# Attention and gated MLP for one decoded token: q made in groups along the steps, W_o in four sets, W_down by plain columns

## The chip, the cores and the metric

The kernel runs on one core of one Trainium2 chip. The metric is device time in microseconds (us) of the whole launch, as the median of several runs. An engine name in what follows is the profile's: PE is TensorE's matmul, PEld its weight load, DVE is VectorE, ACT is ScalarE, POOL is GpSimd, SP is SyncE, which here only issues DMAs.

## The reference, cut to what matters

One token for each of B = 2 sequences goes through a pre-normalised attention with a cache, then through a gated MLP. Everything is bf16 at the interface.

```python
B, D = 2, 512;  Hq = Hkv = 32;  Sk = 8192;  Dh = 128;  F = 1376
q = layernorm(x) @ wq                                # (2, 512) @ (512, 4096)
p = softmax(q . k_cache * Dh**-0.5)                  # per sequence and head, 8192 keys
h = x + concat_heads(p . v_cache) @ wo               # (2, 4096) @ (4096, 512)
n = layernorm(h)
out = h + (relu(n @ W_gate) * (n @ W_up)) @ W_down   # 512 -> 1376 -> 512
```

The two caches hold 2 x 32 x 8192 x 128 elements each, 134 MB apiece. The weights are 4 MB each for wq and wo, and 1.4 MB for each of the three MLP matrices.

## The kernel before, in words

**Steps.** One step handles two heads of one sequence; there are N = 32 steps (`steps`, 16 pairs of heads for each sequence). A step's keys are one 4 MB load, 128 partitions of 128 keys (64 partitions for each head), into one of two slots of `kbuf`; its values are another into one of two slots of `vbuf` (`load_kv`, L118). The order of instructions is written out by hand: each engine runs its own in the order of the code, and all big loads are issued by SP in that order.

**Scores** (`scores`, L255). Of the 128 keys of a partition, 112 are done by DVE: a multiply with the replicated query `qrep` (L290), four halving adds (L297) and a sum (L301). The other 16 go over PE: transposes (L275), copies by ACT (L276), matmuls with `qT` (L266). Then come the row maxima (`pm`, L309), a matmul that spreads them (`mx_ps`, L311), `nm` (L316) and the exponentials on ACT (L319), which write `pgz`. The next step's multiply stands behind `nm` in DVE's order.

**Values** (`values`, L324). The values of step i-1 stand behind the scores of step i on PE: 32 matmuls of 512 columns (L344), or, in the last three steps, 128 matmuls of 128 rows (L333). Every fourth step a group of heads is collected and normalised into `ocol`.

**Loop** (L362 to L369). Step i: `scores(i)`, the load of K(i+2) into the slot that step i has just read, `values(i-1)`, the load of V(i+1) into the slot that those values have read. So a K load is issued when DVE and PE are done with a step's keys, a V load when PE is done with the values.

**Before the loop.** x is normalised, wq is loaded into `wbig`, and q is made in eight groups of four heads (L206 to L214): four matmuls of 512 columns (`q_ps`, L209), a copy by ACT (`qrow`, L213), four matmuls that replicate it over the partitions (`r_ps`, L200), a copy by ACT (`qrep`, L204). After all eight groups, 32 small matmuls make `qT` (L217), and only then come the transposes of step 0 in PE's order.

**After the loop.** SP issues W_o (L377, three pieces of one layout: partition p holds 32 consecutive rows of W_o), W_gate and W_up (L384, into `kbuf` slot 0), W_down (L388, L393, into tiles of its own). Then come the last scores, with the values of step 30 between, the values of step 31, the spreading of `ocol` into W_o's row layout (L407 on DVE, L411 on PE, `orow` L415), 128 matmuls with W_o (L420; the weights are columns at a stride of four elements), the second layernorm (L428 to L436, L456), the two products (L450), `gate` and `hm` (L463, L469), 44 matmuls with W_down (L476, stride four), the residual (L481), four matmuls that turn columns into rows (L485), two copies (L488, L489) and the output DMA (L490).

Of the kernel before, what the change touches and what calls it, by code (L numbers as in the profile page):

```python
# [7 lines left out]
ACT = mybir.ActivationFunctionType  # L8
ALU = mybir.AluOpType
# [14 lines left out]
def kernel(  # L24
# [25 lines left out]
    NG = Hq // 2  # L50
# [6 lines left out]
    bf16 = mybir.dt.bfloat16  # L57
    f32 = mybir.dt.float32

    FULL = F // (2 * P) * 2  # L60
# [1 line left out]
    FC = FULL + 1  # L62


    SETS = [(0, Hq, P, (16, 12, 4))]

    WD = (3, 1, 1)

# [3 lines left out]
    big = ctx.enter_context(tc.tile_pool(name="big", bufs=1))  # L72
    consts = ctx.enter_context(tc.tile_pool(name="consts", bufs=1))
# [5 lines left out]
    pad = big.tile([P, 192], bf16)  # L79
    kbuf = big.tile([P, 2, ROW], bf16)  # L80
    vbuf = big.tile([P, 2, ROW], bf16)
    wbig = big.tile([P, KC * Hq * Dh], bf16)
    wd_sb = big.tile([P, FULL, D], bf16)
    wd_r = big.tile([P, D], bf16)

    wq_sb = wbig.rearrange("p (c n) -> p c n", c=KC)
    wgu = kbuf[:, 0, 0:2 * KC * F].rearrange("p (k c f) -> p k c f", k=2, c=KC)

    qrep = consts.tile([P, B, NG, Dh], bf16)
    qrow = consts.tile([P, Hq * Dh], bf16)  # L90
# [1 line left out]
    zc = consts.tile([P, B, NG, 2], f32)  # L92
    ob = consts.tile([P, T4 * Dh], f32)
    ident = consts.tile([P, P], bf16)
    identf = consts.tile([P, P], f32)
    nscale = consts.tile([P, P], f32)
    ones = consts.tile([P, P], f32)
    mean_w = consts.tile([P, P], f32)
# [2 lines left out]
    eps_col = consts.tile([P, 1], f32)  # L101
    warm = consts.tile([P, 1], f32)
    ocol = consts.tile([P, Hq, B], bf16)
    rows = [m * Dh // pn for _, m, pn, _ in SETS]
    quot = [consts.tile([P, Dh // n], bf16, name=f"quot{k}") for k, n in enumerate(rows)]
    rest = [consts.tile([P, n], bf16, name=f"rest{k}") for k, n in enumerate(rows)]
    orow = [consts.tile([P, n, B], bf16, name=f"orow{k}") for k, n in enumerate(rows)]
# [10 lines left out]
    def load_kv(cache, buf, i, pieces=1):  # L118
        b, g = steps[i]
        w = ROW // pieces  # L120
        for k in range(pieces):
            nc.sync.dma_start(
                out=buf[:, i % 2, k * w:(k + 1) * w],
                in_=_dram(cache, (b * Hkv + 2 * g) * Sk * Dh + k * w, [[ROW, P], [1, w]]),
            )
# [12 lines left out]

    with tc.manual_schedule():

        nc.sync.dma_start(out=wbig, in_=_dram(A_wq, 0, [[KC * Hq * Dh, P], [1, KC * Hq * Dh]]))
        nc.scalar.dma_start(out=xrow[0:B, :], in_=_dram(A_x, 0, [[D, B], [1, D]]))
        load_kv(A_k_cache, kbuf, 0, pieces=2)
        load_kv(A_k_cache, kbuf, 1)
# [10 lines left out]
        nc.gpsimd.memset(pgz, 0.0)  # L155
        nc.gpsimd.memset(zc, 0.0)
        nc.gpsimd.memset(ob, 0.0)
        nc.gpsimd.memset(identf, 0.0)
        select(identf, 1.0, 0, [[-1, P]], 1)

        nc.gpsimd.memset(sel, 0.0)
        for j in range(2):
# [30 lines left out]
        nc.scalar.activation(out=warm, in_=eps_col, func=ACT.Exp)  # L193


        def spread(n):
            r_ps = ps2.tile([P, B, 2, Dh], f32, tag="tp", name="r_ps")
            for b in range(B):
                for j in range(2):
                    nc.tensor.matmul(  # L200
                        out=r_ps[j * HALF:(j + 1) * HALF, b], lhsT=pick[0:B, b, :],
                        rhs=_free(qrow[0:B, :], (4 * n + j) * Dh, [[2 * Dh, 2], [1, Dh]]), start=True, stop=True,
                    )
            nc.scalar.activation(out=qrep[:, :, 2 * n:2 * n + 2, :], in_=r_ps, func=ACT.Copy)  # L204

        for n in range(NG // 2):  # L206
            q_ps = ps2.tile([P, 512], f32, tag="tp")
            for c in range(KC):
                nc.tensor.matmul(  # L209
                    out=q_ps[0:B, :], lhsT=xn[:, c, :], rhs=wq_sb[:, c, n * 512:(n + 1) * 512],  # L210
                    start=(c == 0), stop=(c == KC - 1),
                )
            nc.scalar.activation(out=qrow[0:B, n * 512:(n + 1) * 512], in_=q_ps[0:B, :], func=ACT.Copy)  # L213
            spread(n)  # L214
        qT_ps = ps.tile([P, Hq, B], f32, tag="acc")
        for h in range(Hq):
            nc.tensor.matmul(  # L217
                out=qT_ps[:, h, :], lhsT=qrow[0:B, h * Dh:(h + 1) * Dh], rhs=ident[0:B, 0:B],
                start=True, stop=True,
            )  # L220
        nc.scalar.activation(out=qT, in_=qT_ps, func=ACT.Copy)


        groups = {}
# [137 lines left out]
        for i in range(N - 1):  # L362
            scores(i)
            if i + 2 < N:
                load_kv(A_k_cache, kbuf, i + 2)
            if i >= 1:
                values(i - 1)
            if i + 1 < N:
                load_kv(A_v_cache, vbuf, i + 1, pieces=2 if i + 1 == N - 1 else 1)  # L369

        off = 0
        wo_at = []
        for (h0, m, pn, pieces), n in zip(SETS, rows):
            wo_at.append(off)
            r0 = 0
            for w in pieces:
                nc.sync.dma_start(  # L377
                    out=wbig[0:pn, off + r0 * D:off + (r0 + w) * D],
                    in_=_dram(A_wo, h0 * Dh * D + r0 * D, [[n * D, pn], [1, w * D]]),
                )  # L380
                r0 += w
# [17 lines left out]


        att_ps = ps.tile([P, KC, B], f32, tag="acc")
        for k, (h0, m, pn, _) in enumerate(SETS):
            n = rows[k]
            or_ps = ps.tile([P, B, n], f32, tag="mx")
            for b in range(B):
                sp = small.tile([P, m, Dh // n], bf16, tag="spread")
                nc.vector.tensor_tensor(  # L407
                    out=sp, in0=_free(ocol, h0 * B + b, [[B, m], [0, Dh // n]]),
                    in1=_free(quot[k], 0, [[0, m], [1, Dh // n]]), op=ALU.mult,
                )  # L410
                nc.tensor.matmul(  # L411
                    out=or_ps[0:pn, b, :], lhsT=sp.rearrange("p h q -> p (h q)"), rhs=rest[k],
                    start=True, stop=True,
                )
            nc.vector.tensor_copy(orow[k][0:pn], or_ps[0:pn].rearrange("p b c -> p c b"))  # L415
        for k, (h0, m, pn, _) in enumerate(SETS):
            n = rows[k]
            for r in range(n):
                for c in range(KC):
                    nc.tensor.matmul(  # L420
                        out=att_ps[:, c, :],
                        lhsT=_free(wbig[0:pn, :], wo_at[k] + r * D + c, [[KC, P]]), rhs=orow[k][0:pn, r, :],
                        start=(k == 0 and r == 0 and c == 0),
                        stop=(k == len(SETS) - 1 and r == n - 1), skip_group_check=True,
                    )
# [35 lines left out]
        for r, f in parts:  # L461
            nf = f.stop - f.start
            nc.vector.scalar_tensor_tensor(  # L463
                out=gate[r, f, :], in0=g_ps[r, f, :], scalar=0.0, in1=_free(rvar[r], 0, [[0, nf], [1, B]]),
                op0=ALU.max, op1=ALU.mult,
            )
        product(u_ps, 1)
# [4 lines left out]
        d_ps = ps2.tile([P, KC, B], f32, tag="o")  # L472
        for fc in range(FC):
            w, src = (P, wd_sb[:, fc, :]) if fc < FULL else (LASTW, wd_r[0:LASTW])
            for c in range(KC):
                nc.tensor.matmul(  # L476
                    out=d_ps[:, c, :], lhsT=_free(src, c, [[KC, P]]), rhs=hm[0:w, fc, :],
                    start=(fc == 0 and c == 0), stop=(fc == FC - 1), skip_group_check=True,
                )
        y = small.tile([P, KC, B], bf16, tag="y")  # L480
        nc.vector.tensor_tensor(out=y, in0=d_ps, in1=hc.rearrange("p b c -> p c b"), op=ALU.add)  # L481
        yrow = small.tile([P, KC, P], bf16, tag="yrow")
        yr = [ps2.tile([P, 2, P], f32, tag="tp", name="yr") for _ in range(2)]
        for c in range(KC):
            nc.tensor.matmul(out=yr[c // 2][0:B, c % 2, :], lhsT=y[:, c, :], rhs=ident, start=True, stop=True)  # L485

        by_p = yrow.rearrange("p c q -> p (c q)")
        nc.vector.tensor_copy(_free(by_p[0:B, :], 0, [[1, 2], [KC, P]]), yr[0][0:B])  # L488
        nc.scalar.activation(out=_free(by_p[0:B, :], 2, [[1, 2], [KC, P]]), in_=yr[1][0:B], func=ACT.Copy)  # L489
        nc.sync.dma_start(out=_dram(out, 0, [[D, B], [1, D]]), in_=by_p[0:B, :])  # L490


# [28 lines left out]
```

## Time and profile before

| | us |
|---|---|
| median of 3 runs (lowest, highest) | 665.92 (665.44, 666.05) |
| the profiled execution's own time | 665.44 |
| its span, first to last instruction | 663.7 |
| DVE busy | 547.4 (82%) |
| PE busy | 394.3 (59%) |
| ACT busy | 135.1 (20%) |
| read from HBM | 281.05 MB, 423 GB/s over the span |

All numbers below are from this one execution, in us from the span's start unless said otherwise. Outside the span lie 1.7 us, which belong to the launch. A matmul of two columns is listed with some 170 ns, but they follow each other every 26 to 33 ns, so a run of them is measured from its first start to its last end. The idle time of an engine costs nothing where another one sets the end.

### The profile page before, as it was taken

What the parts mean: (1) busy time and instruction counts of PE and PEld (TensorE: products, weight loads), DVE (VectorE), ACT (ScalarE), POOL (GpSimd) and SP (SyncE); (2) the same over time, 40 slices, a digit from 0 to 9 for tenths busy, and PEclk for the clock granted to TensorE, in tenths of its full rate; (3) what the DMA queues carried; (4) which work ended last, traced back from release to release, by engine and by line L of the source; (5) the groups of instructions that cost most, each with busy time, mean ns of one, the idle gap of its engine ahead of it and who ended that gap; (6) DMA issues with size and microseconds to landing.
All of it is one profiled execution on the core that took longest, in us unless ns stands there. A gap on an engine that the chain in (4) does not pass through costs nothing.

```text
span 663.7 us, 6643 instructions
## 1 busy us (share of the span) xinstructions
PE 394.3 (59%) x2858; PEld 191.6 (29%) x2858; DVE 547.4 (82%) x301; ACT 135.1 (20%) x307; POOL 5.2 (1%) x29
## 2 busy tenths in 40 slices
PE   2763665676656545776456567564577655457555
PEld 1241222333223222322223232232223222223454
DVE  0849999999888899888889987888988888898831
ACT  2340221222202212211221221122122112212100
POOL 3000000000000000000000000000000000000000
PEclk9999888888766778867678886677888667788555
DMA  8999999999999999999999999999999999999995
GB/s 365 454 398 415 404 431 440 429 428 436 433 427 435 436 431 432 436 432 427 437 434 424 437 440 425 428 442 432 422 440 439 421 433 442 428 427 439 422 422 240
DMA packets 11205, 281.48 MB, mean 424 GB/s; under 512 B 1220, under 2 KB 1320, under 8 KB 2088
## 3 DMA queue, kind: packets, MB, share of 16 engines
q1 hardware_dynamic: 11172, 281.06, 98.7%
q8 instruction: 22, 0.36, 0.2%
q14 instruction: 7, 0.06, 0.0%
q10 hardware_dynamic: 4, 0.00, 0.0%
HBM read 281.05 MB, written 0.00 MB: 423 GB/s over the span
## 4 chain that ended last, share of the span: by engine, by line
DMA 48%; DVE 45%; PE 5%; ACT 1%; issue 1%; SPq 0%; DVEq 0%
DMA kbuf<-in_A_k_cache_dram 40%; DVE kbuf L297 21%; DVE kbuf L290 21%; DMA wd_sb<-in_B_W_down_dram 3%; DVE scol L301 3%; DMA vbuf<-in_A_v_cache_dram 3%; PE q_ps L209 2%; DMA wbig<-in_A_wq_dram 2%; PE mx_ps L311 1%; PE r_ps L200 1%; ACT qrow L213 1%; PE o_ps L333 1%; ACT kT L276 0%; DVE pm L309 0%; DVE nm L316 0%
## 5 line engine op out<-in xcount | busy, mean ns | idle before, releaser
L290 DVE TENSOR_TENSOR kbuf<-kbuf,qrep 128x14336 bf16<-128x14336 bf16 (+2 forms) x33 | 244.1, 7397 | 41.5 <-DMA kbuf<-in_A_k_cache_dram 41.5
L344 PE MATMUL po<-vbuf,pgz 128*8 128x512 bf16 x928 | 260.5, 451 | 0.0
L297 DVE TENSOR_TENSOR kbuf<-kbuf 128x7168 bf16<-128x7168 bf16 (+3 forms) x128 | 244.2, 1908 | 4.4
L311 PE MATMUL mx_ps<-nscale,pm 128*128 128x128 f32 x64 | 24.5, 487 | 191.6 <-DVE pm L309 191.6
L344 PEld LDWEIGHTS <-pgz 128*8 128x8 bf16 x928 | 89.5, 99 | 162.9 <-issue 86.2
L319 ACT ACTIVATE pgz<-scol,nm 64x128 bf16<-64x128 f32 x64 | 27.9, 436 | 225.8 <-DVE nm L316 225.0
L311 PEld LDWEIGHTS mx_ps<-nscale,pm 128*128 128x128 f32 x64 | 16.0, 311 | 193.5 <-issue 193.5
L276 ACT ACTIVATE kT<-t_ps 128x1024 bf16<-128x1024 bf16 x64 | 62.1, 1021 | 18.7 <-PE t_ps L275 18.3
L349 ACT ACTIVATE ob<-po 8x512 f32<-8x512 f32 x29 | 17.1, 588 | 218.2 <-PE po L344 218.2
L266 PE MATMUL sc_ps<-qT,kT 128*128 128x2 bf16 x512 | 22.7, 165 | 39.6 <-ACT kT L276 39.6
L275 PE MATMUL t_ps<-ident,kbuf 128*128 128x128 bf16 x512 | 36.5, 228 | 0.0
L301 DVE TENSOR_REDUCE scol<-kbuf 128x112 f32<-128x896 bf16 x32 | 34.8, 1086 | 1.1
L316 DVE TENSOR_REDUCE nm<-mx_ps 128x2 f32<-128x128 f32 x32 | 9.3, 292 | 30.4 <-PE mx_ps L311 30.4
L275 PEld LDWEIGHTS <-kbuf 128*128 128x128 bf16 x512 | 31.8, 104 | 9.2 <-issue 9.1
L266 PEld LDWEIGHTS <-kT 128*128 128x128 bf16 x512 | 17.2, 97 | 48.1 <-ACT kT L276 48.1
L209 PE MATMUL q_ps<-wbig,xn 128*2 128x512 bf16 x32 | 14.9, 621 | 8.4 <-DMA wbig<-in_A_wq_dram 8.4
L309 DVE TENSOR_REDUCE pm<-scol 128x1 f32<-128x128 f32 x32 | 9.1, 283 | 10.0 <-ACT scol L284 7.7
L333 PE MATMUL o_ps<-pgz,vbuf 128*128 128x2 bf16 x384 | 10.7, 165 | 4.6 <-DMA vbuf<-in_A_v_cache_dram 4.6
L333 PEld LDWEIGHTS <-vbuf 128*128 128x128 bf16 x384 | 10.8, 105 | 4.7 <-DMA vbuf<-in_A_v_cache_dram 4.7
L354 PE MATMUL o_ps<-sel,ob 128*128 128x8 f32 (+1 forms) x64 | 8.4, 258 | 5.5 <-ACT ob L349 5.5
L319 ACT ACTIVATION_READ_ACCUMULATOR pgz<-scol,nm 64x1 f32 x64 | 11.7, 182 | 0.0
L354 PEld LDWEIGHTS o_ps<-sel,ob 128*128 128x128 f32 x64 | 7.7, 191 | 9.5 <-ACT ob L349 8.3
(82 smaller groups left out, 83.8 us busy)
## 6 DMA issues: line engine op xcount, KB each, us to landing
kbuf<-in_A_k_cache_dram SPq DMA_DIRECT2D x31, 4096.0 KB, 22.1
vbuf<-in_A_v_cache_dram SPq DMA_DIRECT2D x31, 4096.0 KB, 21.4
wbig<-in_A_wq_dram SPq DMA_DIRECT2D x1, 4096.0 KB, 12.1
kbuf<-in_A_k_cache_dram SPq DMA_DIRECT2D x2, 2048.0 KB, 18.7
vbuf<-in_A_v_cache_dram SPq DMA_DIRECT2D x2, 2048.0 KB, 16.4
wbig<-in_A_wo_dram SPq DMA_DIRECT2D x1, 2048.0 KB, 23.0
wbig<-in_A_wo_dram SPq DMA_DIRECT2D x1, 1536.0 KB
kbuf<-in_B_W_gate_dram SPq DMA_DIRECT2D x1, 1376.0 KB, 30.0
```

Of the source, the lines that this page charges most:

```text
L209: nc.tensor.matmul(out=q_ps[0:B, :], lhsT=xn[:, c, :], rhs=wq_sb[:, c, n * 512:(n + 1) * 512], start=(c == 0), stop=(c == KC - 1),)
L266: nc.tensor.matmul(out=sc_ps[:, t, :], lhsT=kT[:, t * P:(t + 1) * P], rhs=_free(qT, 2 * g * B + b, [[B, 2]]), start=True, stop=True,)
L275: nc.tensor.transpose(t_ps[:, k, :], kt[:, t * Dh:(t + 1) * Dh], ident)
L276: nc.scalar.activation(out=kT[:, c0 * P:(c0 + TPC) * P], in_=t_ps.rearrange("p t s -> p (t s)"), func=ACT.Copy,)
L290: nc.vector.tensor_tensor(out=kv, in0=kv, in1=_free(qrep, (b * NG + g) * Dh, [[0, n], [1, Dh]]), op=ALU.mult,)
L297: nc.vector.tensor_tensor(out=lo, in0=lo, in1=_free(kt, half, [[Dh, NV], [1, half]]), op=ALU.add,)
L301: nc.vector.tensor_reduce(out=scol[:, 0:NV], in_=_free(kt, 0, [[Dh, NV], [1, 8]]), axis=AXIS.X, op=ALU.add,)
L311: nc.tensor.matmul(out=mx_ps.rearrange("p a b -> p (a b)"), lhsT=_free(pm, 0, [[0, P]]), rhs=nscale, start=True, stop=True,)
L319: nc.scalar.activation(out=pgz[r, s, :, j], in_=scol[r, :], func=ACT.Exp, scale=SCALE, bias=nm[r, j:j + 1], accum_out=zc[r, b, g, j:j + 1],)
L333: nc.tensor.matmul(out=o_ps[e][:, 2 * k:2 * k + 2], lhsT=vbuf[:, s, t * Dh:(t + 1) * Dh], rhs=pgz[:, s, t, :], start=(t == 0), stop=(t == ...
L344: nc.tensor.matmul(out=po[e][r, :], lhsT=_free(pgz, s * NT * 2 + u * T4 * 2, [[1, 2 * T4]]), rhs=vbuf[:, s, u * T4 * Dh:(u + 1) * T4 * Dh] ...
L349: nc.scalar.activation(out=ob[r, :], in_=po[e][r, :], func=ACT.Copy)
```

## The change

It has four parts.

1. **q.** `make_q(n)` makes four heads complete: `q_ps`, `qrow`, `r_ps`, `qrep` and now also their four columns of `qT`. Groups 0 and 1 are made ahead of the loop; groups 2 to 7 behind the values of steps 0 to 5.
2. **W_o.** Four sets in place of one: heads 0 to 5 on 48 partitions (0 to 23 and 32 to 55, 16 rows of W_o on each), 16 heads on 128 partitions with 16 rows, 8 heads with 8 rows, 2 heads with 2 rows. Each set has its own load (set 0 has two, with an outermost count of 6), its own constants `rest` and `quot`, its own spreading and `orow`. The last V load is one piece, where it was two.
3. **W_down** is loaded as before, but into `kbuf` behind W_up, and its columns are read side by side.
4. **h in rows.** The residual is laid into rows by four f32 matmuls (`hx`, `fold`), in front of the product with W_up; the MLP's output is copied, turned by one matmul on top of it, copied once, and stored as eight rows of 256 bytes.

```diff
-    SETS = [(0, Hq, P, (16, 12, 4))]
+    WHOLE = ((0, P),)
+    SIX = ((0, 24), (32, 24))
+    SETS = [(0, 6, SIX, 6), (6, 16, WHOLE, 16), (22, 8, WHOLE, 16), (30, 2, WHOLE, 16)]
...
-    wd_sb = big.tile([P, FULL, D], bf16)
+    wd_sb = kbuf[:, 0, 2 * KC * F:2 * KC * F + FULL * D].rearrange("p (f n) -> p f n", f=FULL)
...
-        for n in range(NG // 2):
+        def make_q(n):
             q_ps = ps2.tile([P, 512], f32, tag="tp")
...
-        qT_ps = ps.tile([P, Hq, B], f32, tag="acc")
-        for h in range(Hq):
+            qT_ps = ps.tile([P, 4, B], f32, tag="acc")
+            for h in range(4):
                 nc.tensor.matmul(
...
+        EARLY = 2
+        for n in range(EARLY):
+            make_q(n)
...
             if i + 1 < N:
-                load_kv(A_v_cache, vbuf, i + 1, pieces=2 if i + 1 == N - 1 else 1)
+                load_kv(A_v_cache, vbuf, i + 1)
+            if i + EARLY < NG // 2:
+                make_q(i + EARLY)
...
-        for (h0, m, pn, pieces), n in zip(SETS, rows):
+        for (h0, m, blocks, k), n in zip(SETS, rows):
+            r0 = h0 * Dh
+            for p0, w in blocks:
+                nc.sync.dma_start(
+                    out=wbig[p0:p0 + w, off:off + n * D],
+                    in_=_dram(A_wo, r0 * D, [[w // k * n * D, k], [n * D, w // k], [1, n * D]]),
+                )
+                r0 += w * n
...
+                sp = small.tile([P, P], bf16, tag="spread")
+                if blocks is not WHOLE:
+                    nc.gpsimd.memset(sp, 0.0)
+                h1 = h0
+                for p0, w in blocks:
+                    mb = w // q
                     nc.vector.tensor_tensor(
...
+                nc.tensor.matmul(out=or_ps[0:pn, b, :], lhsT=sp[:, 0:pn], rhs=rest[k], start=True, stop=True)
...
+        hx = small.tile([P, KC, B, KC], f32, tag="hx")
+        nc.vector.tensor_tensor(
+            out=hx, in0=_free(hc, 0, [[1, KC], [KC, B], [0, KC]]), in1=_free(quarter, 0, [[0, KC], [0, B], [1, KC]]),
+            op=ALU.mult,
+        )
+        y_ps = ps2.tile([P, P], f32, tag="tp")
+        for c in range(KC):
+            nc.tensor.matmul(
+                out=y_ps[0:B * KC, bass.DynSlice(c, P // KC, step=KC)],
+                lhsT=hx[:, c].rearrange("p b q -> p (b q)"), rhs=fold, start=(c == 0), stop=False,
...
         product(u_ps, 1)
...
-                    out=d_ps[:, c, :], lhsT=_free(src, c, [[KC, P]]), rhs=hm[0:w, fc, :],
+                    out=d_ps[:, :, c], lhsT=src[:, c * P:(c + 1) * P], rhs=hm[0:w, fc, :],
...
+        nc.vector.tensor_copy(d, d_ps.rearrange("p b c -> p (b c)"))
+        nc.tensor.matmul(out=y_ps[0:B * KC, :], lhsT=d, rhs=ident, start=False, stop=True, skip_group_check=True)
+        y = small.tile([P, P], bf16, tag="y")
+        nc.vector.tensor_copy(y[0:B * KC, :], y_ps[0:B * KC, :])
+        nc.sync.dma_start(out=_dram(out, 0, [[P, B * KC], [1, P]]), in_=y[0:B * KC, :])
```

The loops that build `rest` and `quot` on POOL now run over four sets. The number of selections (`select`, L127) on POOL ahead of the loop goes from 12 in the kernel before to 115 in the new one, most of them for `rest` (8, 8, 16 and 64).

More of the change, by code (lines that the diff above doesn't have):

```diff
@@ L81 @@
     vbuf = big.tile([P, 2, ROW], bf16)
-    wbig = big.tile([P, KC * Hq * Dh], bf16)
-    wd_sb = big.tile([P, FULL, D], bf16)
+    rows = [m * Dh // sum(w for _, w in blocks) for _, m, blocks, _ in SETS]
+    wbig = big.tile([P, max(KC * Hq * Dh, sum(rows) * D)], bf16)
     wd_r = big.tile([P, D], bf16)
-    wq_sb = wbig.rearrange("p (c n) -> p c n", c=KC)
+    wq_all = wbig[:, 0:KC * Hq * Dh]
+    wq_sb = wq_all.rearrange("p (c n) -> p c n", c=KC)
     wgu = kbuf[:, 0, 0:2 * KC * F].rearrange("p (k c f) -> p k c f", k=2, c=KC)
+    wd_sb = kbuf[:, 0, 2 * KC * F:2 * KC * F + FULL * D].rearrange("p (f n) -> p f n", f=FULL)
     qrep = consts.tile([P, B, NG, Dh], bf16)
@@ L94 @@
     ident = consts.tile([P, P], bf16)
-    identf = consts.tile([P, P], f32)
+    fold = consts.tile([P, HALF // 2], f32)
+    quarter = consts.tile([P, KC], f32)
     nscale = consts.tile([P, P], f32)
@@ L103 @@
     ocol = consts.tile([P, Hq, B], bf16)
-    rows = [m * Dh // pn for _, m, pn, _ in SETS]
     quot = [consts.tile([P, Dh // n], bf16, name=f"quot{k}") for k, n in enumerate(rows)]
@@ L139 @@
     with tc.manual_schedule():
-        nc.sync.dma_start(out=wbig, in_=_dram(A_wq, 0, [[KC * Hq * Dh, P], [1, KC * Hq * Dh]]))
+        nc.sync.dma_start(out=wq_all, in_=_dram(A_wq, 0, [[KC * Hq * Dh, P], [1, KC * Hq * Dh]]))
         nc.scalar.dma_start(out=xrow[0:B, :], in_=_dram(A_x, 0, [[D, B], [1, D]]))
@@ L157 @@
         nc.gpsimd.memset(ob, 0.0)
-        nc.gpsimd.memset(identf, 0.0)
-        select(identf, 1.0, 0, [[-1, P]], 1)
+        nc.gpsimd.memset(fold, 0.0)
+        for c in range(KC):
+            select(fold, 1.0, -c * (P // KC), [[-1, P // KC]], 1)
+        nc.gpsimd.memset(quarter, 1.0)
+        select(quarter, 0.0, 0, [[-(P // KC), KC]], 1, ALU.is_ge)
+        select(quarter, 0.0, P // KC - 1, [[P // KC, KC]], -1, ALU.is_ge)
         nc.gpsimd.memset(sel, 0.0)
@@ L193 @@
         nc.scalar.activation(out=warm, in_=eps_col, func=ACT.Exp)
-        def spread(n):
+        def make_q(n):
+            q_ps = ps2.tile([P, 512], f32, tag="tp")
+            for c in range(KC):
+                nc.tensor.matmul(
+                    out=q_ps[0:B, :], lhsT=xn[:, c, :], rhs=wq_sb[:, c, n * 512:(n + 1) * 512],
+                    start=(c == 0), stop=(c == KC - 1),
+                )
+            nc.scalar.activation(out=qrow[0:B, n * 512:(n + 1) * 512], in_=q_ps[0:B, :], func=ACT.Copy)
             r_ps = ps2.tile([P, B, 2, Dh], f32, tag="tp", name="r_ps")
@@ L204, in spread @@
             nc.scalar.activation(out=qrep[:, :, 2 * n:2 * n + 2, :], in_=r_ps, func=ACT.Copy)
-        for n in range(NG // 2):
-            q_ps = ps2.tile([P, 512], f32, tag="tp")
-            for c in range(KC):
+            qT_ps = ps.tile([P, 4, B], f32, tag="acc")
+            for h in range(4):
                 nc.tensor.matmul(
-                    out=q_ps[0:B, :], lhsT=xn[:, c, :], rhs=wq_sb[:, c, n * 512:(n + 1) * 512],
-                    start=(c == 0), stop=(c == KC - 1),
-                )
-            nc.scalar.activation(out=qrow[0:B, n * 512:(n + 1) * 512], in_=q_ps[0:B, :], func=ACT.Copy)
-            spread(n)
-        qT_ps = ps.tile([P, Hq, B], f32, tag="acc")
-        for h in range(Hq):
[L217 to L221, printed above, removed]
+                    out=qT_ps[:, h, :], lhsT=qrow[0:B, (4 * n + h) * Dh:(4 * n + h + 1) * Dh],
+                    rhs=ident[0:B, 0:B], start=True, stop=True,
+                )
+            nc.scalar.activation(out=qT[:, 4 * n:4 * n + 4, :], in_=qT_ps, func=ACT.Copy)
+        EARLY = 2
+        for n in range(EARLY):
+            make_q(n)
         groups = {}
@@ L368 @@
             if i + 1 < N:
-                load_kv(A_v_cache, vbuf, i + 1, pieces=2 if i + 1 == N - 1 else 1)
+                load_kv(A_v_cache, vbuf, i + 1)
+            if i + EARLY < NG // 2:
+                make_q(i + EARLY)
         off = 0
         wo_at = []
-        for (h0, m, pn, pieces), n in zip(SETS, rows):
-            wo_at.append(off)
[L375 to L381, printed above, removed]
+        for (h0, m, blocks, k), n in zip(SETS, rows):
[6 more added lines that the diff above has]
+                r0 += w * n
+            wo_at.append(off)
             off += n * D
@@ L401 @@
         att_ps = ps.tile([P, KC, B], f32, tag="acc")
-        for k, (h0, m, pn, _) in enumerate(SETS):
+        for k, (h0, m, blocks, _) in enumerate(SETS):
             n = rows[k]
+            q = Dh // n
+            pn = sum(blocks[-1])
             or_ps = ps.tile([P, B, n], f32, tag="mx")
             for b in range(B):
[L406 to L414, printed above, removed]
+                sp = small.tile([P, P], bf16, tag="spread")
[5 more added lines that the diff above has]
+                    nc.vector.tensor_tensor(
+                        out=_free(sp, p0, [[q, mb], [1, q]]), in0=_free(ocol, h1 * B + b, [[B, mb], [0, q]]),
+                        in1=_free(quot[k], 0, [[0, mb], [1, q]]), op=ALU.mult,
+                    )
+                    h1 += mb
+                nc.tensor.matmul(out=or_ps[0:pn, b, :], lhsT=sp[:, 0:pn], rhs=rest[k], start=True, stop=True)
             nc.vector.tensor_copy(orow[k][0:pn], or_ps[0:pn].rearrange("p b c -> p c b"))
-        for k, (h0, m, pn, _) in enumerate(SETS):
+        for k, (h0, m, blocks, _) in enumerate(SETS):
             n = rows[k]
+            pn = sum(blocks[-1])
             for r in range(n):
@@ L466 @@
             )
+        hx = small.tile([P, KC, B, KC], f32, tag="hx")
+        nc.vector.tensor_tensor(
+            out=hx, in0=_free(hc, 0, [[1, KC], [KC, B], [0, KC]]), in1=_free(quarter, 0, [[0, KC], [0, B], [1, KC]]),
+            op=ALU.mult,
+        )
+        y_ps = ps2.tile([P, P], f32, tag="tp")
+        for c in range(KC):
+            nc.tensor.matmul(
+                out=y_ps[0:B * KC, bass.DynSlice(c, P // KC, step=KC)],
+                lhsT=hx[:, c].rearrange("p b q -> p (b q)"), rhs=fold, start=(c == 0), stop=False,
+                skip_group_check=True,
+            )
         product(u_ps, 1)
@@ L469 @@
             nc.vector.tensor_tensor(out=hm[r, f, :], in0=gate[r, f, :], in1=u_ps[r, f, :], op=ALU.mult)
-        d_ps = ps2.tile([P, KC, B], f32, tag="o")
+        d_ps = ps2.tile([P, B, KC], f32, tag="o")
         for fc in range(FC):
@@ L476 @@
                 nc.tensor.matmul(
-                    out=d_ps[:, c, :], lhsT=_free(src, c, [[KC, P]]), rhs=hm[0:w, fc, :],
+                    out=d_ps[:, :, c], lhsT=src[:, c * P:(c + 1) * P], rhs=hm[0:w, fc, :],
                     start=(fc == 0 and c == 0), stop=(fc == FC - 1), skip_group_check=True,
                 )
[L480 to L490, printed above, removed]
+        d = small.tile([P, B * KC], bf16, tag="d")
+        nc.vector.tensor_copy(d, d_ps.rearrange("p b c -> p (b c)"))
[3 more added lines that the diff above has]
+        nc.sync.dma_start(out=_dram(out, 0, [[P, B * KC], [1, P]]), in_=y[0:B * KC, :])
 _INS = ['A_x', 'A_k_cache', 'A_v_cache', 'A_wq', 'A_wo', 'B_x', 'B_W_gate', 'B_W_up', 'B_W_down']
```

## The prediction

> **What bounds the kernel now.** I read the page's slices first: the DMA row is at nine tenths or more nearly throughout, while no engine is.
>
> ```profile
> DMA  8999999999999999999999999999999999999995
> HBM read 281.05 MB, written 0.00 MB: 423 GB/s over the span
> ```
>
> So the span is a stream of loads with something ahead of it and something behind. Only three things can move the time: gaps in the stream, its bytes (unchanged), and what follows the last load. I asked for windows around each place where the rate drops (columns: us, busy time and instructions of PE, PEld, DVE, ACT, POOL, then granted clock, DMA share, GB/s).
>
> ```profile
> 13.00:41.00 28.00, 22.35 (x116) 7.76 (x115) 16.50 (x7) 10.87 (x19) 0.00 (x0) 1.00 1.02 438
> 41.00:44.00 3.00, 1.58 (x22) 1.38 (x22) 0.42 (x2) 1.11 (x3) 0.00 (x0) 1.00 1.02 344
> 61.00:64.00 3.00, 2.88 (x8) 1.21 (x9) 2.08 (x2) 0.98 (x4) 0.00 (x0) 1.00 0.95 317
> 71.00:74.00 3.00, 1.77 (x27) 1.17 (x25) 2.97 (x2) 2.43 (x3) 0.00 (x0) 1.00 0.81 279
> 104.00:300.00 196.00, 119.85 (x734) 55.47 (x732) 175.41 (x89) 41.41 (x95) 0.00 (x0) 0.77 1.00 433
> ...
> 654.00:656.00 2.00, 0.75 (x6) 0.66 (x5) 0.74 (x5) 0.00 (x0) 0.00 (x0) 0.50 0.78 303
> 656.00:658.00 2.00, 1.55 (x44) 1.46 (x44) 0.22 (x2) 0.00 (x0) 0.00 (x0) 0.50 0.53 198
> ```
>
> Three gaps stand near 42, 62 and 72; after that the stream runs at 433 GB/s until 654. The timeline of SP's queue says why: after five loads at the start, nothing is issued for 38 us.
>
> ```profile
> 2.76 0.45 SPq L122 DMA_DIRECT2D vbuf<-in_A_v_cache_dram  x1
> 40.66 0.33 SPq L122 DMA_DIRECT2D kbuf<-in_A_k_cache_dram  x1
> 60.65 0.33 SPq L122 DMA_DIRECT2D kbuf<-in_A_k_cache_dram  x1
> 71.44 0.33 SPq L122 DMA_DIRECT2D vbuf<-in_A_v_cache_dram  x1
> ```
>
> K2 waits for PE to transpose slot 0, and those transposes (38.74 to 40.63) stand behind all eight q groups, though DVE was done with the slot at 34.92. DVE then idles 7.7 for the transposed part, and K3 and V2 are late in turn. For the end I read the chain.
>
> ```profile
> 620.91 18.50 DMA vbuf<-in_A_v_cache_dram
> 639.43 19.96 DMA wd_sb<-in_B_W_down_dram
> 659.44 0.57 PE d_ps L476 x12
> 660.25 0.60 PE yr L485 x4
> ```
>
> The last matmuls wait for W_down. And the timeline of the tail prices its parts.
>
> ```profile
> 643.13 0.41 PE L411 MATMUL or_ps<-rest,sp 128*128 128x32 bf16 x2 [0.66 <-DVE sp L407]
> 648.28 2.29 PE L420 MATMUL att_ps<-orow,wbig 128*128 128x2 bf16 x64 [1.69 <-DMA wbig<-in_A_wo_dram]
> 617.28 3.60 PE L333 MATMUL o_ps<-pgz,vbuf 128*128 128x2 bf16 x128
> 608.16 1.05 PE L354 MATMUL o_ps<-sel,ob 128*128 128x2 f32 x8 [0.68 <-ACT ob L349]
> ```
>
> **q: the stream's gaps.** With two groups ahead of the loop, PE is free at 12.98 + 2 x 3.1 (a group, from the chain's spacing) + 0.2 = 19.4; the transposes wait for K0's second half (landed 22.64) and end some 4 us later, far ahead of DVE at 34.92. K2 goes out at 35.0 instead of 40.66, six us before V0 has landed (41.9). Step 1 starts at 36.4 instead of 44.16, so K3 goes out near 53 (V1 lands by 61.5) and V2 near 63.7 (K3 lands by 71.2). Every gap closes. Size: the landing records have 4 MB every 9.71 us from 162.43 to 628.72 (48 loads); K1 to V2 (32.36 to 83.64) took 51.28 for five loads, which should be 48.57. That is **2.7**. The windows say 2.5: 3 x ((432-344) + (432-317) + (432-279)) / 432. I take 2.7, with zero as the other end if something else delays K2.
>
> What is put into steps 0 to 5 issues no DMA. It stands behind `values` on PE and behind the `ob` copy on ACT; queued behind it are the next transposes and `kT` copies, and DVE's `pm` waits for those. Before, PE and ACT had the transposed scores ready 13.2 after `mx_ps` of the step (79.17 to 92.4) while `pm` came at 17.6. A group costs PE 3.1 and ACT's `qT` copy 0.2: 16.5 to 17, still ahead by over half a microsecond, and a late `pm` would first use up six us of lead. Cost nothing. On POOL, 103 selections more at 0.27 (four in 1.07) run until about 33; nobody needs them before 640, since `sel` precedes them. The wait of W_o for the last read of wq and of W_down for slot 0 (DVE done at 616) are over when SP comes there.
>
> **The last values.** Before, they began at 638.92, behind the exponentials; V31's second half landed at 639.41. As one piece it must land whole: 639.41 - 2.7 = 636.7. Call V = 636.75 the new start, 2.17 earlier. Everything below hangs on V.
>
> **W_o.** The values take 3.55 and the normalising 0.3; the first spreading starts at V + 3.87 as before (642.79). One round of spreading took 0.79 to the cast and some 0.2 more to the next: 1.0. Four rounds are serial, since each engine alternates DVE, PE, DVE: 3 x 1.0 + 0.75, so PE is free at V + 7.6. Then 168 matmuls instead of 128, at 33.2 ns (64 in 2.29 less one latency): 5.75, end at V + 13.4 = 650.1. Before it was 650.57, with 2.5 of waiting for W_o inside. The sets' loads land by 646 at the latest and delay nothing.
>
> How long do the loads last? Evenly spread, the last W_down piece lands at 659.4 - 2.7 = 656.7. The shares 0.78 and 0.53 above show that part of the 16 DMA engines has finished early; in the landing records six of the 16 completions of each late load come 2 to 4 ahead of the last. Set 0's outermost count is 6, and the page shows that a load can use fewer engines: the two rows of x left four packets in their queue (q10), two rows and two completions. If only six engines carry set 0, each of those gets 80 KB more and the other ten 48 KB less, at 27 KB per us (128 KB in 4.85): +3.0 and -1.8. If they are the early six, all ends near 655.9; if they are late ones, at 659. [...]
>
> **To the end.** `hc` follows at 650.15, `g` at 651.4 (1.22 to `devb`; the gate weights land by 649), `gate` 2.86 later at 654.3, `hx` at 654.5 (0.17, as the small DVE rows). The four f32 matmuls are eight passes; the nearest row has eight in 1.05, and with u's start behind them I take 0.95. Ends: 0.6, and 3.1 by `mx_ps` (0.77 each, four times the columns). PE's queue behind them holds the product with W_up, which before ran straight behind the second mean and waited for its load only: u starts at 655.4 (its load: by 653). From u's start to W_down's first matmul 1.81, so 657.2. The columns side by side should take the 26.5 ns of L333, not 33: 44 in 1.35, done 658.55. From there before: 1.63 to the output's issue (659.99 to 661.62). Now a copy 0.17, one matmul 0.27, a copy of 8 x 128 at 0.28 (a 128x64 cast took 0.23; the strided one it replaces 0.71) and hand-offs: 0.86. Issue at 659.4; issue to the end of the span was 2.09: **661.5** against 663.7.
>
> **Sum.** -2.2: the profiled 665.44 becomes 663.2. That execution was 0.48 under the median, so I forecast 665.92 - 2.2 = **663.7**. The tail itself is a draw: 24.8 from V to the end in both, the output's gain and W_down's paying for the rounds and the 40 matmuls; the saving is the head's. What was the end (W_down's load) has two to three us of slack in the new one.
>
> **The rivals.**
> - *The extra W_o falls on late DMA engines.* Gate weights land near 652.7 instead of 649, W_down at 659: d ends near 659.9, +1.35, total **665.0**. Only the place of the early six decides, which no view shows.
> - *The head gain stays out.* Something holds DVE in step 0 until past 41.5: then V = 639.46 and the total is **666.4**. For: POOL now runs until 33, beside DVE's big multiplies. Against: small DVE rows beside POOL at 3 to 5 us took 0.17, as in the tail without POOL. At one selection for each of DVE's seven large instructions it is 1.9 in step 0; it decides from 6.5 on. [...]
> - *PE becomes the pace of steps 1 to 5 (slower).* The place is L344, then the q group, then L275. The values' matmuls run at 0.43 for the first eleven, then 0.21. If all ran at 0.43 (the granted clock falls to 0.71 there), values take 13.8, and a step 0.8 + 13.8 + 3.2 + 4.0 = 21.8 against the stream's 19.43. Over five steps V loads fall 12 behind, less what they have spare: some 8 lost, **669.7**. It decides from a step of 20.6. [...]
> - *The f32 matmuls cost as `mx_ps`*: +2.2, **665.9**. 32 columns instead of 128 speak against it.
>
> **How the numbers follow.** Forecast 0.68, late engines 0.10, no head gain 0.10, PE's pace 0.05, f32 price 0.07. Around the forecast: V ± 0.5 (whether one of the 22 instruction fetches of q8, 0.9 each in the trace, delays the last engine), rounds ± 0.4, f32 -0.3 to +0.7, so 662.4 to 664.9. The range 662.4 to 666.2 leaves out PE's pace, half of no head gain, and the edges: under 0.2. A measurement of this kernel can tell about 0.2%, 1.33 us: faster is under 664.6, slower over 667.3. Faster: 0.68 x 0.92 plus 0.04 of the late-engine case, 0.66. Slower: PE's pace and 0.02 of the rest, 0.07. Same 0.27.
>
> **What would show it.** In the profile after: SP's third K load near 35 and no window under 420 GB/s between 40 and 75; K's multiply in step 1 at 36.4; the last values at 636.75 ± 0.5; four rounds to 644.4; att's end near 650.1 without a DMA wait; u released by PE's own order behind the f32 matmuls, not by its load; d without a wait for W_down. The forecast is wrong if a wait for W_down or the gate weights stands in the tail, if V2 is issued after 69, or if the stretch from V to the end differs from 24.8 by over a microsecond.

## The result and the profile after

The forecast was 663.7, faster. The changed kernel measured **668.58** (six runs, 667.06 to 669.32) against 665.70 for the kernel before in the same session (six runs): a ratio of 1.0042, interval 1.0029 to 1.0055. It is slower by 0.4%, and outside the predicted range. Its profiled execution took 668.85, with a span of 667.0 where 661.5 was predicted.

The gain at the head is there. SP's queue after, at the start of the span (start, duration, engine, line, what is issued):

```profile
2.90 0.46 SPq L128 DMA_DIRECT2D vbuf<-in_A_v_cache_dram  x1
...
35.16 0.33 SPq L128 DMA_DIRECT2D kbuf<-in_A_k_cache_dram  x1
53.21 0.33 SPq L128 DMA_DIRECT2D kbuf<-in_A_k_cache_dram  x1
63.24 0.33 SPq L128 DMA_DIRECT2D vbuf<-in_A_v_cache_dram  x1
```

K2, K3 and V2 go out at 35.16, 53.21 and 63.24, where 35.0, 53 and 63.7 were predicted. The windows of the kernel after show the first two gaps closed and the third nearly (371, behind a stretch from 64 to 71 at 449), and where the gain was lost again. The columns are the stretch, its length, the busy time of PE, PEld, DVE, ACT and POOL, the granted clock, the DMA share and the GB/s. A packet is counted, with all its time and bytes, in the window in which it starts, so a short window can show a share over 1.

```profile
41.00:44.00 3.00, 1.26 (x21) 0.83 (x19) 3.00 (x1) 1.99 (x4) 3.00 (x1) 1.00 0.99 426
61.00:64.00 3.00, 3.00 (x15) 1.03 (x13) 2.97 (x2) 0.59 (x1) 2.93 (x2) 1.00 0.96 415
71.00:74.00 3.00, 2.43 (x7) 1.02 (x8) 2.01 (x4) 0.98 (x4) 2.52 (x8) 0.50 0.86 371
...
625.00:632.00 7.00, 4.00 (x130) 3.92 (x130) 6.90 (x4) 0.00 (x0) 0.00 (x0) 0.50 1.01 433
632.00:636.00 4.00, 0.77 (x2) 0.50 (x2) 2.73 (x7) 0.12 (x1) 0.00 (x0) 0.50 1.10 262
636.00:640.00 4.00, 0.58 (x2) 0.50 (x2) 0.00 (x0) 0.86 (x4) 0.00 (x0) 0.50 0.93 182
640.00:644.00 4.00, 2.50 (x94) 2.51 (x95) 0.00 (x0) 0.00 (x0) 0.00 (x0) 0.50 0.97 221
```

The three windows at the head moved 344, 317 and 279 GB/s before. The last three were these before:

```profile
632.00:636.00 4.00, 0.77 (x15) 0.68 (x12) 3.86 (x7) 0.00 (x0) 0.00 (x0) 0.50 1.02 430
636.00:640.00 4.00, 2.30 (x45) 2.04 (x46) 0.36 (x2) 0.98 (x4) 0.00 (x0) 0.50 0.99 420
640.00:644.00 4.00, 2.88 (x95) 2.59 (x92) 0.96 (x5) 0.00 (x0) 0.00 (x0) 0.50 1.00 423
```

After, they move about half as much, **with the DMA engines as busy as ever** (0.93 to 1.10): each packet takes longer. In the records a 16 KB packet of this stretch mostly takes 1.0 to 1.5 where it took 0.61, and a 32 KB packet of V31 takes 2.0 to 2.8 where it took 1.21. Against the 424 that the three windows had on average before, what is missing is 4 x ((424 - 262) + (424 - 182) + (424 - 221)) / 424 = 5.7 us of the stream. The chain of waits and the timeline of the tail show what that did.

```profile
619.06 27.01 DMA wbig<-in_A_wo_dram
...
646.09 17.47 DMA kbuf<-in_B_W_down_dram
...
663.60 0.50 PE d_ps L509 x12
```

```profile
641.50 3.57 PE L345 MATMUL o_ps<-pgz,vbuf 128*128 128x2 bf16 x128 [3.97 <-DMA vbuf<-in_A_v_cache_dram]
...
648.71 5.92 PE L440 MATMUL att_ps<-orow,wbig 56*128 56x2 bf16 x168
...
657.03 1.55 PE L470 MATMUL g_ps<-devb,kbuf 128*128 128x2 bf16 x44 [1.54 <-DMA kbuf<-in_B_W_gate_dram]
...
660.05 0.60 PE L495 MATMUL y_ps<-fold,hx 128*8 128x32 f32 x8 [1.04 <-DVE hx L489]
...
660.58 1.54 PE L470 MATMUL u_ps<-devb,kbuf 128*128 128x2 bf16 x44
...
662.39 1.00 PE L509 MATMUL d_ps<-hm,kbuf 128*128 128x2 bf16 x32 [0.27 <-DVE hm L502]
...
664.95 0.31 SPq L518 DMA_DIRECT2D out_dram<-y  x1
```

The number in brackets is idle time, with what ended it. The last values wait 3.97 for V31, which was issued before set 0, and the end is again a wait for W_down, with set 0's second load (landed 646.07) ahead of it in the chain: SP issued the third piece of W_down right behind that landing, at 646.09. The DMA engines had other loads to move meanwhile (their share stays at 0.92 or more until 658). They did not finish together: the sixteen completions of that piece lie between 655.86 and 663.55, 7.7 apart, where those of the same piece before lay 4.7 apart. Each of set 0's two loads lands with 12 records (634.38 to 643.49 and 636.68 to 646.07, besides one right at its issue), where a load on 128 rows has 16 and that of x, two rows, has two besides the one at its issue. No record names an engine; here and below I read one landing record as one of the 16 DMA engines that the page counts. So twelve carried set 0, not six and not sixteen.

### The profile page after: what moved, and what is told of

The parts are those of the page before. It is cut to its first block, busy times and chain, and to the rows that moved or that the text cites. A ratio compares the mean times of both kernels' runs of the same rounds, so it can differ in the third digit from the quotient of the medians.

```text
span 667.0 us, 6968 instructions
## 1 busy us (share of the span) xinstructions
PE 390.6 (59%) x2909; PEld 193.1 (29%) x2909; DVE 549.0 (82%) x313; ACT 134.7 (20%) x313; POOL 81.9 (12%) x141
## 4 chain that ended last, share of the span: by engine, by line
DMA 53%; DVE 40%; POOL 4%; issue 1%; PE 1%; POOLq 0%; SPq 0%; DVEq 0%
DMA kbuf<-in_A_k_cache_dram 46%; DVE kbuf L309 18%; DVE kbuf L302 18%; DMA wbig<-in_A_wo_dram 4%; POOL rest L134 4%; DVE scol L313 3%; DMA kbuf<-in_B_W_down_dram 3%; PE o_ps L345 1%; PE mx_ps L323 0%; POOLq L134 0%; POOL quot L134 0%; POOL fold L134 0%; SPq L128 0%; DVE nm L328 0%; PE d_ps L509 0%
## 5 line engine op out<-in xcount | busy, mean ns | idle before, releaser
L134 POOL TENSOR_SCALAR_AFFINE_SELECT rest<-rest 128x2 bf16<-128x2 bf16 (+2 forms) x96 | 74.8, 779 | 6.6
L210 PE MATMUL q_ps<-wbig,xn 128*2 128x512 bf16 x32 | 10.7, 469 | 8.1 <-DMA wbig<-in_A_wq_dram 8.1
```

Of the source, the lines that this page charges most:

```text
L134: nc.gpsimd.affine_select(out=t, in_=t, compare_op=op, fill=fill, base=base, pattern=pattern, channel_multiplier=mult,)
```

## The experiments

Set 0's load was the suspect. The theories, by the letters of the expectations:

- **P**: set 0 lies on too few partitions, so its bytes crowd there and hold up whatever is beside them.
- **U**: a load on fewer than 16 DMA engines leaves the sharing of the queue uneven.
- **R**: the number of rounds and loads, or V31 as one piece, costs the time.
- After the second group P was sharpened into **O**: each DMA engine has partitions of its own, those that it writes in a load of 128 rows, and a load that makes it write another engine's slows down both. Its rival there is **F**: a dozen engines or more on fewer than 128 partitions are slow by their number.

### Four sets, all on 128 partitions

```diff
-    SETS = [(0, 6, SIX, 6), (6, 16, WHOLE, 16), (22, 8, WHOLE, 16), (30, 2, WHOLE, 16)]
+    SETS = [(0, 4, WHOLE, 16), (4, 16, WHOLE, 16), (20, 8, WHOLE, 16), (28, 4, WHOLE, 16)]
```

> The changed kernel with four W_o sets that all lie on 128 partitions (4, 16, 8 and 4 heads), so without the set on 48 partitions; all else, the four rounds of spreading and V31 in one piece included, as in the changed kernel. Theory P (set 0's loads crowd onto few partitions, and all packets that go there share their narrow way into SBUF): the rate between 632 and 644 stays at 420 GB/s or more, V31 lands near 637, the time is 663.5 (662.5 to 664.5), five under the changed kernel. Theory U (a load that runs on fewer than 16 DMA engines is what slows the stream): the same here, 663.5. Theory R (the rounds, the number of loads or V31 as one piece cost it): 668, as the changed kernel.

Measured: **661.99** (661.94 to 662.24), ratio to the kernel before 0.9936 [0.9924, 0.9948]. Its windows, and three lines of its chain:

```profile
632.00:636.00 4.00, 0.77 (x2) 0.50 (x2) 2.94 (x7) 0.00 (x0) 0.00 (x0) 0.50 0.97 408
636.00:640.00 4.00, 2.81 (x91) 2.81 (x92) 0.04 (x1) 0.98 (x4) 0.00 (x0) 0.50 1.00 426
```

```profile
645.00 4.28 PE att_ps L440 x128
...
655.68 0.25 DVE hm L502 x2
655.93 1.32 PE d_ps L509 x44
```

The slow stretch is gone, and from the last scores on no DMA is in the chain: all 44 matmuls with W_down run in one piece behind `hm`. Four sets, four rounds and V31 in one piece do not bring it about, so R falls. The loss belongs to set 0's load. The run came out 0.5 under the range that P and U gave. It does less work at one place: sets of 4, 16, 8 and 4 heads need 128 matmuls with W_o and not 168, 4.4 in place of 5.9 in the timelines, and they are in its chain. So by estimate 1.5 of the 6.6 between it and the kernel after are these matmuls, and about 5 are set 0's load.

### Set 0 on 48 partitions side by side

```diff
-    SIX = ((0, 24), (32, 24))
+    SIX = ((0, 48),)
```

> The changed kernel with set 0 as one load of 48 rows onto partitions 0 to 47 (three for each of 16 engines) in place of two loads of 24 rows onto 0 to 23 and 32 to 55. Theory P: still crowded, packets of set 0 and of V31 beside it take 1.5 to 2 times their 0.61 and 1.21, V31 lands 2 to 5 late, 666 to 669. Theory U: all 16 engines carry it, so 663.5.

Measured: **668.5** (668.33 to 669.04), 1.0035 [1.0022, 1.0047], like the kernel after. Its load completes with 16 records, so U falls: all sixteen engines carry it, and its windows are as slow. P's 666 to 669 holds.

```profile
632.00:636.00 4.00, 0.77 (x2) 0.50 (x2) 2.45 (x6) 0.42 (x2) 0.00 (x0) 0.50 1.08 233
636.00:640.00 4.00, 0.58 (x2) 0.50 (x2) 0.00 (x0) 0.56 (x4) 0.00 (x0) 0.50 1.00 193
```

### The kernel before with q in groups, and with the sets

The first takes `make_q`, its two early groups and its six calls in the loop, and nothing else. The second takes part 2 alone (V31 stays in two pieces, and W_down moves into `kbuf`, since `wbig` grows, but is still read at a stride).

```diff
...
+            if i + EARLY < NG // 2:
+                make_q(i + EARLY)
```

> The kernel before with part 1 alone (two q groups ahead of the loop, six behind the steps). Its tail stays as before and stays bound by the stream. Theory P, U and R alike: the three early gaps close and everything after moves up by 2.7, so 663.0 (662.6 to 663.6). If the head's gain were eaten later in the stream, 665.7.

> The kernel before with part 2 alone (four W_o sets, one on 48 partitions; W_down behind W_up in kbuf; V31 still in two pieces). Theory P and U: the slow stretch of some 12 us appears, the stream ends some 5 to 6 later and the time is 670 to 672. Theory R with V31's one piece as its cause: near 667; with the rounds as its cause: 667 to 668, and no slow stretch in the DMA rows.

Measured: q alone **662.67** (662.54 to 662.91), 0.9945 [0.9933, 0.9957]; the sets alone **673.23** (671.2 to 676.24), 1.0104 [1.0079, 1.0129]. So q gives 3.7 and the sets take 6.9, over a microsecond more than the 670 to 672 that was expected. With the sets alone the slow stretch is there too (217 and 221 GB/s from 636 to 644), and the chain has the load of W_up:

```profile
635.21 29.64 DMA kbuf<-in_B_W_up_dram
...
664.89 1.56 PE u_ps L460 x44
```

### Six engines, as the diff suggests

The source of each of set 0's loads is written as six steps of 64 KB, each of four steps of 16 KB (one partition's share). One outer step equals four inner ones, so both counts are one uniform run of 24. Here the source is permuted so that the two counts can't merge.

```diff
-                    in_=_dram(A_wo, r0 * D, [[w // k * n * D, k], [n * D, w // k], [1, n * D]]),
+                    in_=_dram(A_wo, r0 * D, [[n * D, k], [k * n * D, w // k], [1, n * D]] if w == 24 else
+                              [[w // k * n * D, k], [n * D, w // k], [1, n * D]]),
```

> The changed kernel with the rows of set 0's two loads taken in another order (row block e + 6j to partition 4e + j), so that the two outer counts of the source, 6 and 4, cannot be merged into 24; as a result the W_o rows of heads 0 to 5 are misplaced, which changes what is computed. Same bytes, same 48 partitions. Theory P with 12 engines in two on each group of four partitions as the cause: now six engines carry it, each with four partitions of its own, set 0's packets take 0.61 to 0.8 and V31 lands near 637; 662.5 to 664.5. Theory U: fewer engines still, so as slow as the changed kernel or slower, 668 to 671.

Measured: **664.36** (663.26 to 664.64), 0.9964 [0.995, 0.9977]. Each load now has six landing records, and the stretch is at full rate, as P had it; U, which wanted 668 to 671, falls again (windows, then two lines of the chain):

```profile
632.00:636.00 4.00, 0.76 (x2) 0.50 (x2) 2.71 (x7) 0.15 (x1) 0.00 (x0) 0.50 0.95 406
636.00:640.00 4.00, 3.09 (x102) 3.09 (x102) 0.00 (x0) 0.83 (x4) 0.00 (x0) 0.50 1.00 421
```

```profile
641.45 17.72 DMA kbuf<-in_B_W_down_dram
...
659.21 0.49 PE d_ps L510 x12
```

Its chain still ends on W_down, which lands at 659.17, as in the rival of the late engines (659, total 665.0). In its landing records three of set 1's sixteen completions stand ahead of the rest (637.1 to 637.2, the others from 639.8), where late loads of before had six: it seems that half of the loaded engines had been early ones.

### Set 0's bytes on 108 partitions

```diff
+                if w == 24:
+                    e = w * n * D // 108
+                    nc.sync.dma_start(
+                        out=wbig[0:108, off + p0 // 32 * e:off + p0 // 32 * e + e],
+                        in_=_dram(A_wo, r0 * D, [[e, 108], [1, e]]),
+                    )
...
```

> The changed kernel with set 0's bytes loaded in two loads of 108 rows of 3640 bytes onto partitions 0 to 107 (108 is divided by 12 and not by 16, as is 24); the W_o rows of heads 0 to 5 are misplaced, which changes what is computed. Theory P: 12 engines again, but spread over nearly all partitions: packets at full rate, 663 to 664.5. Theory U: 12 engines, so slow, 667 to 669.

Measured: **666.45** (666.11 to 667.54), 1.0006 [0.9997, 1.0015]. Neither theory had it: P wanted full rate, U the loss of before. The stretch is slow by less (272, 249 and 289 GB/s; 16 KB packets about 1.0), and the last values start at 639.64. Spreading over more partitions helps only partly, so P as it stood falls.

### The kernel after with one set, as before

Part 2 undone, parts 1, 3 and 4 kept, V31 in two pieces.

```diff
-    SETS = [(0, 6, SIX, 6), (6, 16, WHOLE, 16), (22, 8, WHOLE, 16), (30, 2, WHOLE, 16)]
+    SETS = [(0, Hq, P, (16, 12, 4))]
...
```

> The changed kernel with W_o as before (one set, three pieces, V31 in two pieces); q, W_down and the rows of h as changed. All theories: no crowding, one round, 128 matmuls; the stream ends near 657, the shorter output saves 0.8 behind it: 662.3 (661.8 to 663.2). If the f32 matmuls in front of the product with W_up set the end, 663.5.

Measured: **662.05** (661.88 to 662.27), 0.9934 [0.9922, 0.9947]. Against q alone (662.67, another session, so by the ratios 0.9934 and 0.9945) parts 3 and 4 add some 0.7 at most; the intervals overlap.

### Where an engine writes

Three runs test O against F. The first is the six-engine load (its source permuted as above) with its partitions moved by 64: same source, same bytes, six landing records for each load again:

```diff
-                    out=wbig[p0:p0 + w, off:off + n * D],
+                    out=wbig[p0 + 64 * (w == 24):p0 + 64 * (w == 24) + w, off:off + n * D],
```

> As the run with set 0 on six engines (rows in another order, so W_o's rows of heads 0 to 5 are misplaced and what is computed changes), and its two blocks moved from partitions 0 and 32 to 64 and 96. Still six engines and 48 partitions, four to an engine. Theory O (each DMA engine has partitions of its own, those it writes in a 128-row load; an engine that writes into another one's partitions shares that one's way in, and both slow down): the six now write where six others are writing V31 and the next set, so packets take 1 to 1.4 (16 KB) and 2 to 2.8 (32 KB) again and the time is 667 to 670. Theory F (it is 12 or more engines on few partitions that slows them): as on six engines, 664.4.

The second and third are the 108-partition load with 96 rows (96 stands for 108 in the destination and in the count too), and with rows shortened to 3,584 bytes. Against the run with 108 rows:

```diff
-                    e = w * n * D // 108
+                    e = w * n * D // 96
...
-                    e = w * n * D // 108
+                    e = w * n * D // 108 // 128 * 128
```

> The changed kernel with set 0's bytes as two loads of 96 rows of 4096 bytes onto partitions 0 to 95 (16 divides 96, so all 16 engines, six rows each); W_o's rows of heads 0 to 5 are misplaced, which changes what is computed. Theory O: six rows to an engine are not the rows it owns, so packets slow down as in the 108-row run, 665.5 to 667. Theory F: 16 engines on 96 partitions are neither few engines nor few partitions, 663 to 664.5.

> The 108-row run with rows of 3584 bytes in place of 3640, so that every row begins at a multiple of 256 bytes; a little of set 0 is left out and its rows are misplaced, which changes what is computed. If odd starts were what slowed that run: packets at full rate, 663.5. Theory O: unchanged, 666.4.

Measured: six engines moved by 64, **671.53** (670.82 to 673.78), 1.0077 [1.0049, 1.0105], where F wanted 664.4; 96 rows, **665.95** (665.72 to 666.15), 0.9994 [0.9983, 1.0004], where F wanted 663 to 664.5; even 108 rows, **666.3** (665.57 to 666.85), 0.9996 [0.9985, 1.0008], so the odd row length of 3,640 bytes played no part. O had 667 to 670, 665.5 to 667 and 666.4. The windows of the first:

```profile
632.00:636.00 4.00, 0.77 (x2) 0.50 (x2) 2.84 (x7) 0.01 (x1) 0.00 (x0) 0.50 1.14 262
636.00:640.00 4.00, 0.59 (x2) 0.50 (x2) 0.00 (x0) 0.97 (x4) 0.00 (x0) 0.50 0.94 195
640.00:644.00 4.00, 2.54 (x95) 2.55 (x96) 0.00 (x0) 0.00 (x0) 0.00 (x0) 0.50 0.95 205
```

All shapes together (the two middle windows are those from 636 to 640 and 640 to 644; V is the start of the last values):

| set 0's loads | engines (by landing records), rows each | GB/s in the two middle windows | V | median |
|---|---|---|---|---|
| four sets on 128 rows | 16, 8 | 426, 412 | 637.63 | 661.99 |
| 24 rows each, six engines, from partitions 0 and 32 | 6, 4 | 421, 419 | 637.36 | 664.36 |
| the same, from partitions 64 and 96 | 6, 4 | 195, 205 | 641.46 | 671.53 |
| the kernel after | 12, 2 | 182, 221 | 641.50 | 668.58 |
| 48 rows side by side | 16, 3 | 193, 211 | 641.43 | 668.5 |
| 108 rows (odd; even) | 12, 9 | 249, 289; 248, 285 | 639.64; 639.97 | 666.45; 666.3 |
| 96 rows | 16, 6 | 261, 307 | 639.81 | 665.95 |

The second and third rows differ in the destination's partitions alone, and that turns full rate into half. So here the placement is the cause, and not the number of engines, of rows or of partitions, and F falls. That it is also the cause in the other slow rows, where the number of engines differs too, is the reading that fits all of them; no run isolates it there. Which partitions are an engine's own, or whether any are, no trace here shows: O's reason for the difference stays my guess, and it fits the runs in so far as only the first two rows of the table are fast (412 to 426 GB/s; the others 182 to 307).

How a misplaced load slows the others is open. O as I put it slows the engine that is misplaced and the one that it intrudes on. In the run moved by 64 all 41 large packets that start between 634 and 638 took the doubled time (some 13 KB per us each, none at 27), and at every moment of that stretch at least sixteen packets were in flight, as in the fast stretches; yet only six engines carried set 0, and by O only six others were to be intruded on. That run came out above O's own 667 to 670. With all traffic at half rate and set 0 on six engines alone, its second load landed at 651.01, which fits the excess but was not tested apart.

## Why the prediction was wrong

**Right, the head.** Most late loads landed 2.5 to 2.8 earlier (159.82 for 162.43, 471.11 for 473.60; 2.7 predicted), though those of a stretch in the middle and the last K load came only 1.5 earlier (617.53 for 619.06). Step 1's multiply began at 36.64 (36.4), and q alone is worth 3.7 between the medians and 2.8 between the spans (660.9 for 663.7), with the end again on W_down, landed at 656.55 where it was 659.4.

**Right, the hand-offs of the tail.** From V: spreading at +3.89 (3.87), PE free for W_o at +7.2 (7.6, since a round took 0.89 and not 1.0), the 168 matmuls done at +13.1 (13.4), u's start to d's start 1.81 (1.81), d's 32 columns in 1.00 (the 26.5 ns), d to the output's issue 0.86 (0.86), issue to the end 2.05 (2.09). The f32 matmuls took 0.53 to u's start, not 0.95. V itself would have come 0.6 to 0.9 later than my 636.75 even without the slow stretch (637.36 and 637.63 above): step 31's multiply began only 1.5 earlier than before (617.55 for 619.08), and the scores, not V31, were then the last to arrive. That multiply waits for the last K load, of which fifteen completions came by 616.20 and the sixteenth at 617.53. An instruction fetch (queue q8) that begins at 609.6 and takes 0.95 may be what held that engine up; the prediction had allowed 0.5 for such a fetch, and that this one did it is not shown.

**Wrong: "The sets' loads land by 646 at the latest and delay nothing."** That sentence, and the paragraph under it that treats set 0 as bytes divided over engines at 27 KB per us, is the step that failed. I weighed six engines against an even spread, and both were off the case: twelve engines carried the load, and it and every load beside it moved at about half the 27 KB per us. V31 had been given the time of before less 2.7 (636.7) though set 0 was queued right behind it; it landed at 641.45, 4.75 later. W_down had 656.7, or 659 with the worst rival; it landed at 663.55. The last set landed at 653.72 and not by 646, the gate weights at 656.98 and not by 649. Both waits that the prediction named as signs of being wrong stand in the tail: 1.54 for the gate weights and one for W_down. The rest of the sum held, so the error of the span, 667.0 - 661.5 = 5.5, is d's end (664.09 for 658.55): 4.75 came with V, 0.44 between V and d's start (the gate weights, less what the hand-offs saved) and 0.35 inside d (W_down). The "two to three us of slack" for W_down did not follow from the prediction's own terms either: 656.7 against a last piece needed 32 matmuls after 657.2, at 658.05, is 1.35.

**The number of engines.** I took the outermost count, 6, from the source as written. The landing records show 12 for each of set 0's loads, whose two counts are one uniform run of 24, and six only when the counts could not merge. Loads of 108 rows came with 12 as well, those of 48, 96 and 128 rows with 16.

**The rivals.** That of the late engines came near in price, 665.0 for 664.36, but its condition was met only in the run with six engines, and there for about half of the load. Some of that is luck: its own terms, 656.7 and 3.0, make 659.7 and not the 659 that it took. None of the four had a load that slows its neighbours. PE's pace of steps 1 to 5 (from one `mx_ps` to the next they took 18.0 to 19.5, where that rival had 21.8), the loss of the head gain and the dear f32 matmuls did not occur.

**POOL.** I let the selections run until about 33; they ran until about 90, and those for `rest` took 779 ns on average (group lines of the kernel after: busy time, mean ns, idle time before):

```profile
L302 DVE TENSOR_TENSOR kbuf<-kbuf,qrep 128x14336 bf16<-128x14336 bf16 (+2 forms) x33 | 244.1, 7398 | 47.3 <-DMA kbuf<-in_A_k_cache_dram 47.3
...
L134 POOL TENSOR_SCALAR_AFFINE_SELECT rest<-rest 128x2 bf16<-128x2 bf16 (+2 forms) x96 | 74.8, 779 | 6.6
```

DVE's multiply has the mean of before (7,397 ns). Of those 96 selections, 21 ran beside one of DVE's multiplies or halving adds and ended 0.04 to 0.05 behind that instruction (one took from 18.26 to 22.53, beside a multiply from 18.06 to 22.49); they took 0.59 to 7.67. The other 75 took 0.19 to 0.20; just one of them touched a multiply, by 0.14. DVE paid nothing, and nobody was held up by POOL: the list of waits puts 9.3 before step 0's `mx_ps` down to a selection, but `nm` came 0.95 behind `pm`, as before (0.95). The 1.9 that I reckoned for step 0 did not appear.

## What to carry to other kernels

In these runs a load's price was not its bytes over the number of engines: where its rows fell decided too (664.36 and 671.53 for the same load at two places), and a small misplaced load (0.8 of 281 MB) halved the rate of everything in flight, also of what was issued before it. Count the landing records of a load before reasoning about its engines, and look at GB/s beside the DMA share: here a share of 0.93 to 1.10 at 182 to 262 GB/s came of 16 KB packets that took 1.0 to 1.5 in place of 0.61, and not of a queue that ran dry. Of the shapes tried, loads on 128 rows kept the rate (426 and 412 GB/s) and gave the best time: sets on 128 rows (and 40 matmuls fewer with them) turned 668.58 into 661.99, level with 662.05 for W_o in one set. Nearly all of that gain over the kernel before is q's: q alone has 662.67.

## What the hardware showed that I had not expected

- Packets that ran at 27 KB per us ran at some 13 while the load moved by 64 was in flight (all 41 large ones that started between 634 and 638; in the kernel after all 40, at 12 to 15), and were back when such a load had landed (in the kernel after, set 0's last load landed at 646.07, and of the large packets that start from 646 to 648, 68 of 70 ran at over 24).
- The same bytes, with six landing records for each load, ran at full rate onto partitions from 0 and 32 (421 and 419 GB/s) and at half onto those from 64 and 96 (195 and 205).
- POOL's selections for `rest` took 779 ns on average, since the 21 that ran beside DVE's multiplies and halving adds took up to 7.67 us, and 215 ns in the kernel before, where they were four and done ahead of the loop; DVE lost nothing.
